# Decay attention and a squared-ReLU feed-forward on one core: the second product of two tiles in seven block products, attention of three tiles in two, and a new order

## The chip, the cores and the metric

The kernel runs on 1 core of one Trainium2 chip. The metric is device time in microseconds of one execution; lower is better. PE is the matrix engine (TensorE), PEld its weight loads, DVE VectorE, ACT ScalarE, POOL GpSimd, SP the engine that issues DMAs.

## What is computed

```python
q, k, v: (4, 8, 768, 64) float32    # batch, heads, sequence, head size
for each block of 64 positions:      # carried state kv_state (batch, head, 64, 64)
    intra = einsum('bhic,bhjc->bhij', qb, kb) * Dmask        # lam**(i-j), lower triangle
    intra = einsum('bhij,bhjd->bhid', intra, vb)
    inter = einsum('bhid,bhde->bhie', qb * lam_pow, kv_state)
    out[block] = intra + inter
    kv_state = lam_block * kv_state + einsum('bhsd,bhse->bhde', kb * rev_pow, vb)
x = out as (3072, 512)               # tokens x (heads * head size)
h = maximum(x @ w_in, 0)             # w_in (512, 2048)
result = (h * h) @ w_out             # w_out (2048, 512)
```

## The kernel before

**Tiles and stages.** The 3072 tokens are 24 chunks of 128 tokens of one sequence, in seven tiles of 2, 3, 3, 4, 4, 4, 4 chunks. For each tile the attention gives x, and the feed-forward part then runs over 16 blocks of 128 hidden features. Values are split into a high and a low part of type fp32r, and a product is three: high by high, high by low, low by high.

**Feed-forward, tiles 0 to 2** (`ffn`, matmuls L633 and L639 to L642): plain products.

**Feed-forward, tiles 3 to 5** (`seven`): eight steps p of two feature blocks. The first product is made of seven block products (L760, 42 matmuls of 128x256 in each step: 2 x 12, then 12 and 6, two block products to a row of twelve) from sums of blocks of x (`combine`, L722 and L725) and sums of blocks of w_in (`sums`, additions on POOL at L696), which are stored in DRAM (`wd`) and streamed back in each step. The second product is plain (L808, 24 matmuls of 128x512 in each step, into four PSUM banks, one for each chunk).

**Feed-forward, tile 6** (`seven2`, `finish`): the first product in the same seven blocks (L875). The second product in seven block products as well (L976, 42 matmuls of 128x256 in each step), except the last step, which is plain in 48 matmuls of 128x256 (L951). The sums of w_out blocks come from `sums2` (L835 to L849) by way of DRAM (`wq`). Seven of the eight PSUM banks hold sums here, so each block product is read out before the next; `finish` (L997) combines the seven sums.

**Attention** (`unit`, `turn_over`): one unit for each chunk. Its *front* (L455, L462) makes the scores and the update of the state; its *values* are the product with the old states (`old64`, L471) and with the masked scores (`values64`, L478). All are matmuls of 64x64, four side by side, recorded as two rows each. One *turn* on PE is the front of a unit and the values of the one before it, as one planned operation. It needs four banks: two for the front (read by DVE at L559 and L565), two for the values, in separate column ranges (read by ACT at L587, added by DVE at L588, multiplied by the decay at L589). In `seven` with its four banks of sums and two of products, a turn takes the place of the product banks, between steps p and p+1 for p = 0, 2, 4, 6 of tiles 3, 4 and 5.

**What sets the order.** Every operation of the program is entered in a `Plan` with an engine, a duration, a key, what it waits for (`deps`), what it only follows (`after`) and the buffers it takes (`SLOTS` gives how many there are of each kind). `Plan.order` lists them by these planned durations, by free buffers and by key, and puts filler matmuls (L321) where PE would be idle before 45 us. A table `EARLY` overrides single keys. The program is then issued in that order on each engine.

Of the kernel before, what the change touches and what calls it, by code (L numbers as in the profile page):

```python
# [19 lines left out]
P = 128  # L20
C = 128
# [17 lines left out]
PLAIN = 3  # L39
Q = 2 * C  # L40
# [19 lines left out]
class Plan:  # L60
# [120 lines left out]

KEY1, KEY2 = (0.0, 3.0), (6.0, 9.0, 14.0)
# [11 lines left out]
POOL_LAT = 2.0  # L194

ISSUE, BEFORE, BEHIND_DMA = 0.45, 1.85, 0.3

EARLY = (
# [28 lines left out]
def kernel(ctx: ExitStack, tc: tile.TileContext, pn, lamx, w, out):  # L227
# [4 lines left out]
    wd = [dram.tile([P, WP], U32, name=f"wd{p}") for p in range(NF // 2)]  # L232
    wdt = [dram.tile([P, 8 * Q], U32, name=f"wq{p}") for p in range(NF // 2)]
# [38 lines left out]
    const.tile([P, 48], F32, name="space")  # L272
# [16 lines left out]
    tiles["ee"] = [t.rearrange("p a b -> p (a b)")[:, 0:DM] for t in tiles["in"]]  # L289
# [241 lines left out]
    def unit(b, c, x, col, key, span, behind=None, vd_act=False, alone=False, raw=None):  # L531

        late = raw is not None or not alone
        t, tv, vd, s1, xr = Buf("in"), Buf("in"), Buf("vds" if late else "half"), [Buf("s1") for _ in range(R)], raw or Buf("xr" if late else "half")
# [41 lines left out]
        def both():  # L576
            old64(t, states, ys)
            values64(vd, s1, ys)

        def back(o_y):  # L580
            def x4(b):
                if raw is None:
                    return at(b).rearrange("p (n i) -> p n i", n=NP)
                i = col // Q * C
                return at(b).rearrange("p (h c i) -> p h c i", h=2, c=NCC)[:, col // C % 2, :, i:i + C]

            oc = [add("ACT", 0.27, 1, lambda r=r: nc.scalar.copy(x4(xr)[:, 2 * r:2 * r + 2], at(ys[r])[:, 0:2 * C].rearrange("p (v i) -> p v i", v=2)), [o_y], [ys[r], xr], f"yi{r}") for r in range(R)]  # L587
            oa = [add("DVE", 0.36, 1, lambda v=v: nc.vector.tensor_tensor(out=by_v(x4(xr), v), in0=y_(ys, v), in1=by_v(x4(xr), v), op=ALU.add), oc, [ys[v], xr]) for v in range(2)]  # L588
            xo = add("DVE", 0.6, 1, lambda: nc.vector.tensor_tensor(out=x4(xr), in0=x4(xr), in1=rdec, op=ALU.mult), oa + o_rdec, [xr])  # L589
            if raw is not None:  # L590
                return [xo]
            cs, n = slice(col, col + C), x.n
            oh = add("ACT", 0.55, 1, lambda: nc.scalar.copy(x_(x, 0, n)[:, :, cs], x4(xr)), [xo], [xr, x])
# [5 lines left out]
        buf_v, dur_v = ys + [t, vd, x or raw, old, mid] + s1, 1.0  # L599
        if alone:  # L600
            o_sc = add("PE", dur_f + EDGE, 0, front, dep_f, buf_f, "sc")
            so = begin_(o_sc)
            return back(add("PE", dur_v + EDGE, 1, both, so + [o_vd] + o_old, buf_v, "y"))
        return dict(key=key, front=Part(dur_f, front, dep_f, buf_f), begin=begin_, values=Part(dur_v, both, [o_vd] + o_old, buf_v), back=back)
# [3 lines left out]
    def rows_out(ti, j, o_done, os_, key):  # L608
# [3 lines left out]
        ob = Buf("vds" if ti >= len(TILES) - 2 and j >= nt - 2 else "ob")  # L612
# [70 lines left out]
    def sums(p, key):  # L683
# [31 lines left out]
    def combine(ti, ready, raw, xc, before, key):  # L715

        A = {n: (lambda i=i: at(raw)[:, 2 * i * Q:2 * (i + 1) * Q]) for i, n in enumerate(("A11", "A12", "A21", "A22"))}
        tmp = Buf("sum")
# [28 lines left out]
    def seven(ti, p, xc, d, os_, key, behind, carry):  # L747

        st, X, Y, u, big, gp = Buf("st"), Buf("bank"), Buf("bank"), Buf("u"), Buf("big"), Buf("gp")
        o_st = plan.op("SP", 5.2, key - 2.5 * 2 * FAST, lambda: nc.sync.dma_start(out=words(at(st)), in_=wd[p]), stored[p], [st], behind + [last_mm.get("stream")])  # L750
# [102 lines left out]
    def seven2(ti, p, xc, d, acc, key, cleared):  # L853
# [6 lines left out]
        for i in range(2):  # L860
            for n in range(1 + p % 2) if not lastp else ():
                m0, m1 = (0, 4) if p % 2 == 0 else ((0, 3), (3, 4))[n]
                o_wt.append(plan.op("SP", 0.36 * (m1 - m0), key - 1.0 * FAST, lambda i=i, n=n, m0=m0, m1=m1: nc.sync.dma_start(
                    out=words(at(wt)[i][n][0]), in_=wdt[p].rearrange("p (a m q) -> p a m q", a=2, m=4)[:, i, m0:m1]), stored2[p], [wt], [o_st] + cleared + last_mm.get("wt", [])))
# [52 lines left out]
        o_12 = tt(0.33, 0.25, lambda: q_(fm, 3), lambda: q_(uq, 3), lambda: q_(bw, 0), ALU.add, [g4], [uq, bw, fm])  # L917
# [69 lines left out]
    def finish(ti, acc, done, key):  # L987

        rows = TILES[ti][0][0] * S + TILES[ti][0][1] * C
        assert [b * S + c * C for b, c in TILES[ti]] == [rows + i * C for i in range(4)]  # L990
        dst = out[rows:rows + 4 * C].rearrange("(i h p) (d m) -> p h d i m", h=2, p=C, d=2)
# [8 lines left out]
        def store(o, b, h, d, i=slice(0, 2)):  # L1000
            plan.op("SP", 0.4 * (i.stop - i.start), key, lambda: nc.sync.dma_start(
                out=dst[:, h, d, i], in_=at(b).rearrange("p (i m) -> p i m", i=2)[:, i]), [o], [b])
# [13 lines left out]
        done[end, 3].after.append(o)  # L1016
# [14 lines left out]
    raws = [Buf("raw") if ti >= PLAIN else None for ti in range(len(TILES))]  # L1031
# [5 lines left out]
    def turn_over(u):  # L1037

        if u is None:
# [152 lines left out]
```

## Time and profile before

| | us |
|---|---|
| three runs | 583.09, 583.12, 583.37 |
| median | 583.12 |
| profiled execution, first to last instruction (span) | 582.5 |
| PE busy | 575.6 |
| VectorE / ScalarE / POOL busy | 435.0 / 266.9 / 29.4 |
| last matmul's end to the span's end, about | 3 |

Of the profiled execution only the span is on hand; the median of the runs is 0.6 us above it. A matmul's row in the trace lasts longer than the distance to the next one, since matmuls overlap; the pace of PE is read from the starts, or from the chain, where overlaps are cut off. The tiles follow one another: the first large product starts at about 19 us, tile 3 at 217, tile 6 at 495.8, and PE's last matmul at about 579.

### The profile page before, as it was taken

The numbers are of one execution on the slowest core, as the hardware profiler recorded it, in microseconds if no ns is written. First come the engines' busy times: TensorE is split into PE (matmuls) and PEld (weight loads), VectorE is DVE, ScalarE is ACT, GpSimd is POOL, SyncE is SP. The second block draws the span as 40 slices with busy tenths as digits, with TensorE's granted clock in tenths as the row PEclk, the third lists the DMA queues.
The fourth block names the chain that finished last, engine by engine and source line by source line (L and its number), as shares of the span: only waits on it lengthen the run. The fifth ranks groups of instructions, "written<-read, shape, count | busy, mean of one in ns | idle before, by whom it ended". The sixth has DMA issues, their size and how long they took to land.

```text
span 582.5 us, 14628 instructions
## 1 busy us (share of the span) xinstructions
PE 575.6 (99%) x6180; PEld 523.3 (90%) x6180; DVE 435.0 (75%) x917; ACT 266.9 (46%) x576; POOL 29.4 (5%) x28
## 2 busy tenths in 40 slices
PE   7999999999999999999999999999999999999997
PEld 6899898889889899888988989889989898999997
DVE  6899999877999786355479667578776548775666
ACT  5887777635434453322235334234442235553452
POOL 2000000100344200000000000000000000000000
PEclk9999999999999999999999999999999999999999
DMA  8846567866788844656454985767777665698722
GB/s 307 278 156 196 188 192 236 280 229 225 272 315 303 341 182 177 214 201 262 181 199 148 362 280 218 274 245 267 255 293 252 231 213 203 198 366 293 260 62 72
DMA packets 36673, 137.26 MB, mean 236 GB/s; under 512 B 3328, under 2 KB 13568, under 8 KB 31488
## 3 DMA queue, kind: packets, MB, share of 16 engines
q1 hardware_dynamic: 36608, 136.34, 66.3%
q8 instruction: 48, 0.79, 0.5%
q14 instruction: 17, 0.14, 0.1%
HBM read 108.01 MB, written 28.31 MB: 234 GB/s over the span
## 4 chain that ended last, share of the span: by engine, by line
PE 94%; DMA 3%; DVE 2%; issue 0%; ACT 0%
PE bank L808 21%; PE bank L760 19%; PE bank L633 15%; PE bank L875 7%; PE bank L976 6%; PE bank L639 5%; PE bank L642 5%; PE bank L640 5%; DMA in<-pn 2%; PE bank L455 2%; PE bank L471 2%; PE bank L478 2%; PE bank L462 1%; DMA halfs<-pn 1%; PE bank L321 1%; PE bank L951 1%
## 5 line engine op out<-in xcount | busy, mean ns | idle before, releaser
L760 PEld LDWEIGHTS bank<-xall,win 128*128 128x128 f32 x1008 | 125.5, 188 | 4.7 <-DVE gs L781 0.7
L808 PE MATMUL bank<-woh,win 128*128 128x512 f32 x384 | 129.0, 394 | 0.0
L760 PE MATMUL bank<-xall,win 128*128 128x256 f32 x1008 | 127.9, 281 | 0.2
L633 PE MATMUL bank<-xall,win 128*128 128x384 f32 (+1 forms) x576 | 93.2, 318 | 0.0
L633 PEld LDWEIGHTS bank<-xall,win 128*128 128x128 f32 x576 | 90.2, 188 | 1.6
L808 PEld LDWEIGHTS bank<-woh,win 128*128 128x128 f32 x384 | 72.0, 188 | 14.6
L808 PE MATMUL bank<-wol,win 128*128 128x512 f32 x192 | 75.2, 392 | 0.0
L639 PE MATMUL bank<-woh,ghs 128*128 128x512 f32 x128 | 50.6, 395 | 0.0
L640 PE MATMUL bank<-wol,ghs 128*128 128x512 f32 x128 | 49.9, 390 | 0.0
L875 PE MATMUL bank<-xall,win 128*128 128x256 f32 x336 | 43.9, 280 | 0.0
L875 PEld LDWEIGHTS bank<-xall,win 128*128 128x128 f32 x336 | 41.6, 188 | 0.2
L808 PEld LDWEIGHTS bank<-wol,win 128*128 128x128 f32 x192 | 36.1, 188 | 5.6
L642 PE MATMUL bank<-woh,gls 128*128 128x512 f32 x128 | 35.9, 392 | 0.5 <-issue 0.5
L792 DVE TENSOR_TENSOR ms<-gs,bank 128x512 f32<-128x512 f32 x24 | 16.5, 686 | 25.6 <-PE bank L760 25.2
L780 ACT COPY gs<-bank 128x256 f32<-128x256 f32 x24 | 9.0, 374 | 57.7 <-PE bank L760 56.1
L649 ACT ACTIVATE gs<-bank 128x384 f32<-128x384 f32 (+1 forms) x48 | 21.9, 455 | 29.3 <-PE bank L633 28.3
L696 POOL TENSOR_TENSOR ms<-win 128x512 f32<-128x512 f32 x16 | 25.2, 1584 | 168.2 <-DVE wol L391 109.4
L799 ACT CAST win<-ms 128x512 fp32r<-128x512 f32 x24 | 14.9, 620 | 40.0 <-DVE ms L798 40.0
L656 DVE TENSOR_TENSOR gls<-gs,ghs 128x384 fp32r<-128x384 f32 (+1 forms) x48 | 28.7, 601 | 5.8 <-ACT ghs L652 5.0
L976 PE MATMUL bank<-woh,win 128*128 128x256 f32 x148 | 32.4, 284 | 0.0
L642 PEld LDWEIGHTS bank<-woh,gls 128*128 128x128 f32 x128 | 23.6, 188 | 5.5 <-issue 0.9
L639 PEld LDWEIGHTS bank<-woh,ghs 128*128 128x128 f32 x128 | 24.0, 188 | 4.9
(144 smaller groups left out, 958.4 us busy)
## 6 DMA issues: line engine op xcount, KB each, us to landing
win<-wd SPq DMA_DIRECT2D x32, 1792.0 KB, 8.3
in<-pn SPq DMA_DIRECT2D x44, 512.0 KB, 6.9
in<-w SPq DMA_DIRECT2D x32, 512.0 KB, 3.9
wd<-xall SPq DMA_DIRECT2D x8, 1024.0 KB, 4.9
out<-obs SPq DMA_DIRECT2D x20, 256.0 KB, 4.0
wd<-win SPq DMA_DIRECT2D x8, 512.0 KB, 6.3
wq<-win SPq DMA_DIRECT2D x7, 512.0 KB, 10.4
wq<-gls SPq DMA_DIRECT2D x7, 512.0 KB, 10.8
```

What stands on the lines that cost most here:

```text
L633: nc.tensor.matmul(at(h)[:, 0:n], wt[:, cc, :], xt[:, cc, 0:n], start=k == 0, stop=k == 3 * NCC - 1)
L639: nc.tensor.matmul(at(os_[j]), gh_()[:, sl], woh[f], start=f == 0, stop=False)
L640: nc.tensor.matmul(at(os_[j]), gh_()[:, sl], wol[f], start=False, stop=False)
L642: nc.tensor.matmul(at(os_[j]), gl_()[:, sl], woh[f], start=False, stop=f == NF - 1)
L649: orr = plan.op("ACT", ta, key - ahead, lambda: nc.scalar.activation(g_(), at(h)[:, 0:n], AF.Relu), [o1], [h, turn_, g])
L656: ogl = plan.op("DVE", tv, key - ahead, lambda: nc.vector.tensor_tensor(out=gl_(), in0=g_(), in1=gh_(), op=ALU.subtract), [og, ogh], [g, g ...
L696: oa = [plan.op("POOL", 1.1, key, lambda f=f, m=m: nc.gpsimd.tensor_tensor(out=at(m), in0=whole(f)[0], in1=whole(f)[1], op=ALU.add), list( ...
L760: nc.tensor.matmul(at(to)[:, i * Q:(i + 1) * Q], wt[a][:, cc, :], xt[b][:, cc, :], start=first and k == 0, stop=stop and k == 5, skip_grou ...
L792: c12 = dve(0.6, 0.7, lambda: nc.vector.tensor_tensor(out=quarter(big, 0, 2).rearrange("p (n i) -> p n i", n=2), in0=quarter(u, 1).unsquee ...
L808: nc.tensor.matmul(at(os_[j]), a, wt[2 * p + k], start=first and part == 0 and wt is woh, stop=p == NF // 2 - 1 and part == 1 and not firs ...
L875: nc.tensor.matmul(at(to)[:, i * Q:(i + 1) * Q], wts[a][:, cc, :], xt[b][:, cc, :], start=i == 0 and k == 0, stop=k == 5, skip_group_check ...
L976: nc.tensor.matmul(at(acc[m])[:, i * Q:(i + 1) * Q], a, block(wn, wp), start=p == 0 and i == 0 and part == 0 and wp == 0, stop=p == NF // ...
```

## The change

1. **Tile 5 takes the form of tile 6.** Tiles from `BOTH2 = 5` on run `seven2` and `finish`. `sums2` therefore moves one tile ahead, to tiles 3 and 4. Tile 6 has its own buffers for x (`raw2`, in the four input buffers) and for a temporary (`sum2`).
2. **Attention of tiles 4, 5, 6 within tiles 3 and 4.** The 12 turns stand behind steps 0, 1, 2, 4, 5, 6 of tiles 3 and 4 (`TURNS`). The results of tiles 5 and 6 go to DRAM (`xd`: eight stores) and come back before their tile (`fetch`: five loads).
3. **Values in one bank.** `values64` adds the product of the masked scores onto the columns that `old64` wrote. It does so in two halves: *straight* (same row half of the array as `old64`, issued with it as an operation of its own) and *cross* (the other row half), issued behind the next unit's front. Between them stands `fence`, a ScalarE copy of 64x2 elements of the bank, which cross waits for. The two copies L587 and the additions L588 go; two multiplications of 128x256 from the banks stay.
4. **Sums of w_in.** The 16 additions of POOL are on DVE.
5. **Order.** Some `after` are `deps` now, a planned DMA latency is longer, and `EARLY` is another table (about a hundred other keys).

```diff
+BOTH2 = 5
+TURNS = [(ti, p) for ti in (3, 4) for p in (0, 1, 2, 4, 5, 6)]
...
+BETWEEN = 0.8
...
-POOL_LAT = 2.0
-
-ISSUE, BEFORE, BEHIND_DMA = 0.45, 1.85, 0.3
+ISSUE, BEFORE, BEHIND_DMA = 0.45, 1.85, 0.5
...
 EARLY = (
-    (2, 0.7), (9, 26.4), (12, 38.4), (36, 22.2), (38, 14.4), (47, 42), (48, -64), (56, 40.4),
+    (3, -59), (6, 56), (7, -6), (14, -1013.1), (22, -723), (26, 183), (30, -1007), (35, -7),
...
-    def values64(vd, s1, ys):
-        for r in range(R):
-            for j in range(2):
-                for v, e in QUARTERS:
-                    i = (2 + r) * C + j * TW
-                    nc.tensor.matmul(
-                        at(ys[v])[half(e), i:i + TW], heads(at(vd))[half(v), head(r, j, e)], s64(s1[r])[half(v), e * 2 + j],
-                        start=False, stop=True, skip_group_check=True)
+    def values64(vd, s1, ys, cross):
+        for j in (1, 0) if cross else (0, 1):
+            for v, e in QUARTERS:
+                r = v ^ cross
+                nc.tensor.matmul(
+                    at(ys[r])[half(e), v * C + j * TW:v * C + j * TW + TW], heads(at(vd))[half(v), head(r, j, e)], s64(s1[r])[half(v), e * 2 + j],
+                    start=False, stop=True, skip_group_check=True)
+
+    def fence(ys, dep, key):
+        o = plan.op("ACT", 0.1, key, lambda: nc.scalar.copy(seen[0:TW], at(ys[1])[0:TW, TW:2 * C:C]), [dep], ys)
+        return o, plan.op("NONE", 0.0, key, lambda: None, [o], lat=-BETWEEN)
...
-            oc = [add("ACT", 0.27, 1, lambda r=r: nc.scalar.copy(x4(xr)[:, 2 * r:2 * r + 2], at(ys[r])[:, 0:2 * C].rearrange("p (v i) -> p v i", v=2)), [o_y], [ys[r], xr], f"yi{r}") for r in range(R)]
-            oa = [add("DVE", 0.36, 1, lambda v=v: nc.vector.tensor_tensor(out=by_v(x4(xr), v), in0=y_(ys, v), in1=by_v(x4(xr), v), op=ALU.add), oc, [ys[v], xr]) for v in range(2)]
-            xo = add("DVE", 0.6, 1, lambda: nc.vector.tensor_tensor(out=x4(xr), in0=x4(xr), in1=rdec, op=ALU.mult), oa + o_rdec, [xr])
+            xo = [add("DVE", 0.36, 1, lambda r=r: nc.vector.tensor_tensor(
+                out=x4(xr)[:, 2 * r:2 * r + 2], in0=at(ys[r])[:, 0:2 * C].rearrange("p (v i) -> p v i", v=2), in1=rdec[:, 2 * r:2 * r + 2], op=ALU.mult), [o_y] + o_rdec, [ys[r], xr]) for r in range(R)]
...
+            if staged is not None:
+                dst = staged.rearrange("p (h n i) -> p h n i", h=2, n=NP)[:, col // C % 2, :, col // Q * C:col // Q * C + C]
+                return [add("SP", 0.75, 1, lambda: nc.sync.dma_start(out=dst, in_=x4(xr)), xo, [xr])]
...
+        first = Part(0.75, straight, [o_vd] + o_old, ys + [t, vd, x or xr, old, mid] + s1)
+        second = Part(0.25, cross, [], ys + [vd] + s1)
...
-        oa = [plan.op("POOL", 1.1, key, lambda f=f, m=m: nc.gpsimd.tensor_tensor(out=at(m), in0=whole(f)[0], in1=whole(f)[1], op=ALU.add),
-                      list(ws[f][0]), [m], lat=POOL_LAT) for f, m in ((f0, ma), (f1, mb))]
+        oa = [plan.op("DVE", 0.6, key, lambda f=f, m=m: nc.vector.tensor_tensor(out=at(m), in0=whole(f)[0], in1=whole(f)[1], op=ALU.add),
+                      list(ws[f][0]), [m]) for f, m in ((f0, ma), (f1, mb))]
...
         if pending:
-            p, so, dest = pending[0]
-            deps, bufs, dur = deps + so + p["values"].deps, bufs + p["values"].bufs, dur + p["values"].dur
...
+            p, so, dest = pending.pop()
+            one, two = p["values"]
+            begun = in_turn("both", plan.op("PE", one.dur, key, one.fn, so + one.deps, one.bufs))
+            fns, deps, bufs, dur = fns + [two.fn], deps + [fence(p["ys"], begun, key)[1 if f else 0]], bufs + two.bufs, dur + two.dur
+        o = in_turn("both", plan.op("PE", dur, key, lambda: [fn() for fn in fns], deps, list({id(b): b for b in bufs}.values())))
...
-            if ti == len(TILES) - 1:
+            if ti >= BOTH2:
```

**PE, one turn in tile 3.** Before, the end of a front (L462) and the start of the values behind it (L471 is `old64`); wide matmuls stand ahead of the front and behind the values alone.

```order
L462 MATMUL bank_83<-halfs,in_97 64x64
L462 MATMUL bank_82<-halfs,in_97 64x64
L462 MATMUL bank_83<-halfs,in_97 64x64
L471 MATMUL bank_81<-in_100,hold_94 64x64
L471 MATMUL bank_79<-in_100,hold_94 64x64
L471 MATMUL bank_81<-in_100,hold_94 64x64
```

Now, the end of the straight half (L470, `values64`), then six matmuls of the plain second product (L812), then the front (L448).

```order
L470 MATMUL bank_86<-s_2_105,halfs 64x64
L470 MATMUL bank_83<-s_3_106,halfs 64x64
L812 MATMUL bank_85<-woh,win 128x512
L812 MATMUL bank_85<-wol,win 128x512
L812 MATMUL bank_84<-woh,win 128x512
L812 MATMUL bank_84<-wol,win 128x512
L812 MATMUL bank_85<-woh,win 128x512
L812 MATMUL bank_84<-woh,win 128x512
L448 MATMUL bank_81<-in_101 64x64
L448 MATMUL bank_88<-in_101 64x64
```

The turn's matmuls, one run before, are two runs now, with six wide matmuls between them.

**DVE, one turn in tiles 3 to 5.** Before: masks of the front (L559), the values (L588, L589), the states (L565, L572), then a weighting (L493), ahead of the next step's first read of a product (L781, not shown).

```order
L800 TENSOR_TENSOR win<-ms,win 128x512
L559 TENSOR_TENSOR s_2_103<-bank_82,mask 128x256
L559 TENSOR_TENSOR s_3_104<-bank_83,mask 128x256
L588 TENSOR_TENSOR halfs<-bank_81,halfs 128x2x128
L588 TENSOR_TENSOR halfs<-bank_79,halfs 128x2x128
L565 TENSOR_TENSOR hold_91<-bank_82,hold_95 128x128
L589 TENSOR_TENSOR halfs<-halfs,rdec 128x4x128
L565 TENSOR_TENSOR hold_91<-bank_83,hold_95 128x128
L565 TENSOR_TENSOR hold_93<-bank_82,hold_91 128x128
L565 TENSOR_TENSOR hold_93<-bank_83,hold_91 128x128
L572 TENSOR_TENSOR hold_93<-hold_93,tables 128x256
```

Now, in tile 3: two multiplications of the values (L587), masks (L556), states (L562, L569), with `sums2` (L841) between.

```order
L804 TENSOR_TENSOR win<-ms,win 128x512
L587 TENSOR_TENSOR obs<-bank_86,rdec 128x256
L587 TENSOR_TENSOR obs<-bank_83,rdec 128x256
L556 TENSOR_TENSOR s_2_105<-bank_81,mask 128x256
L556 TENSOR_TENSOR s_3_106<-bank_88,mask 128x256
L562 TENSOR_TENSOR hold_93<-bank_81,hold_96 128x128
L562 TENSOR_TENSOR hold_93<-bank_88,hold_96 128x128
L562 TENSOR_TENSOR hold_97<-bank_81,hold_93 128x128
L562 TENSOR_TENSOR hold_97<-bank_88,hold_93 128x128
L841 TENSOR_TENSOR obs<-woh,wol 128x512
L569 TENSOR_TENSOR hold_97<-hold_97,tables 128x256
```

The values are read first now, in two operations, and sums of w_out blocks stand among the states.

**PE, from tile 5 to tile 6.** Before: the plain second product of tile 5 (L808, its banks 84, 85, 86, 80), and tile 6's first block products (L875).

```order
L808 MATMUL bank_80<-woh,win 128x512
L808 MATMUL bank_84<-woh,win 128x512
L875 MATMUL bank_79<-xall,win 128x256 x12
L875 MATMUL bank_81<-xall,win 128x256 x12
L875 MATMUL bank_83<-xall,win 128x256 x12
L875 MATMUL bank_82<-xall,win 128x256 x6
L808 MATMUL bank_85<-woh,win 128x512
L808 MATMUL bank_85<-wol,win 128x512
```

Now: the plain last step of tile 5 (L955), the rest of tile 6's first step and the second step's block products (L879), each into a bank of its own, then tile 6's sums (L980).

```order
L955 MATMUL bank_86<-woh,gls 128x256
L955 MATMUL bank_86<-woh,win 128x256
L955 MATMUL bank_86<-wol,win 128x256
L955 MATMUL bank_86<-woh,ghs 128x256
L879 MATMUL bank_83<-xall,win 128x256 x12
L879 MATMUL bank_85<-xall,win 128x256 x6
L879 MATMUL bank_88<-xall,win 128x256 x12
L879 MATMUL bank_87<-xall,win 128x256 x12
L879 MATMUL bank_82<-xall,win 128x256 x12
L980 MATMUL bank_81<-woh,win 128x256
```

The products behind the hand-over take banks that tile 5's sums have just left (83, 85, 88, 87, 82).

## Rows read from the trace of the kernel before

**Rows 1.** The page: busy time by engine; granted clock in 40 slices.
```profile
PE 575.6 (99%) x6180; PEld 523.3 (90%) x6180; DVE 435.0 (75%) x917; ACT 266.9 (46%) x576; POOL 29.4 (5%) x28
...
PEclk9999999999999999999999999999999999999999
```
**Rows 2.** The page: share of engines in the chain that ended last.
```profile
PE 94%; DMA 3%; DVE 2%; issue 0%; ACT 0%
```
**Rows 3.** Stretches (start:end length): PE, PEld, DVE, ACT, POOL busy (x count), clock, DMA.
```profile
100.00:215.00 115.00, 114.54 (x1454) 103.06 (x1453) 98.84 (x207) 52.71 (x110) 25.19 (x16) 1.00 0.77 274
...
310.00:402.00 92.00, 91.88 (x1022) 82.37 (x1021) 65.78 (x141) 35.18 (x73) 0.00 (x0) 1.00 0.74 261
...
509.00:573.00 64.00, 64.00 (x538) 63.94 (x537) 43.08 (x89) 31.25 (x68) 0.00 (x0) 1.00 0.65 226
```
**Rows 4.** Waits of PE's weight loads: releaser, us in total, times, longest.
```profile
PEld bank L455 <- issue: 6.1, 18, 0.4
```
**Rows 5.** The chain in order of time: start us, us, what.
```profile
231.02 2.76 PE bank L808 x12
...
520.60 1.45 PE bank L976 x12
522.04 1.42 PE bank L875 x12
...
573.71 5.77 PE bank L951 x48
```
**Rows 6.** PE's timeline around one turn: start us, us, line, operation, count.
```profile
247.13 0.63 PE L808 MATMUL bank<-woh,win 128*128 128x512 f32 x2
...
248.20 0.65 PE L462 MATMUL bank<-halfs,in 64*64 64x64 f32 x32
248.67 0.65 PE L471 MATMUL bank<-in,hold 64*64 64x64 f32 x32
...
249.71 0.50 PE L808 MATMUL bank<-woh,win 128*128 128x512 f32 x1
250.05 0.40 PE L808 MATMUL bank<-wol,win 128*128 128x512 f32 x1
```
**Rows 7.** The same around a lone front.
```profile
113.74 0.61 PE L642 MATMUL bank<-woh,gls 128*128 128x512 f32 x2
114.28 0.69 PE L455 MATMUL bank<-in 64*64 64x64 f32 x32
...
115.38 0.50 PE L639 MATMUL bank<-woh,ghs 128*128 128x512 f32 x1
115.71 0.39 PE L640 MATMUL bank<-wol,ghs 128*128 128x512 f32 x1
```
**Rows 8.** PE's timeline, start: idle ahead in square brackets; L321 are fillers.
```profile
10.29 0.90 PE L446 MATMUL bank<-s,halfs 64*64 64x128 f32 x32 [0.66 <-DVE s L513]
11.12 0.70 PE L321 MATMUL bank<-obs 128*128 128x256 f32 x2
...
13.66 0.90 PE L432 MATMUL bank<-in 64*64 64x128 f32 x32 [0.94 <-DMA in<-pn]
...
20.53 2.75 PE L321 MATMUL bank<-obs 128*128 128x256 f32 x12
```
**Rows 9.** Groups by line and shape: busy us, mean ns | idle ahead, releaser.
```profile
L696 POOL TENSOR_TENSOR ms<-win 128x512 f32<-128x512 f32 x16 | 25.2, 1584 | 168.2 <-DVE wol L391 109.4 <-DVE xall L705 58.9
...
L588 DVE TENSOR_TENSOR halfs<-bank,halfs 128x256 f32<-128x256 f32 x40 | 15.4, 419 | 3.6 <-ACT halfs L587 3.6
...
L799 ACT CAST win<-ms 128x512 fp32r<-128x512 f32 x24 | 14.9, 620 | 40.0 <-DVE ms L798 40.0
...
L589 DVE TENSOR_TENSOR halfs<-halfs,rdec 128x512 f32<-128x512 f32 x20 | 13.7, 684 | 0.1
...
L587 ACT COPY halfs<-bank 128x256 f32<-128x256 f32 x40 | 12.9, 375 | 16.0 <-PE bank L478 16.0
```

More of the change, by code (lines that the diff above doesn't have):

```diff
@@ L232 @@
     wd = [dram.tile([P, WP], U32, name=f"wd{p}") for p in range(NF // 2)]
+    xd = {ti: dram.tile([P, 4 * 512], F32, name=f"xd{ti}") for ti in range(BOTH2, len(SIZES))}
     wdt = [dram.tile([P, 8 * Q], U32, name=f"wq{p}") for p in range(NF // 2)]
@@ L288 @@
     tiles["fm"] = [flat["m"][:, 0:6 * Q]]
-    tiles["ee"] = [t.rearrange("p a b -> p (a b)")[:, 0:DM] for t in tiles["in"]]
+    tiles["ee"], tiles["raw2"] = ([t[:, k] for t in tiles["in"]] for k in range(2))
+    tiles["raw2"] = [tiles["raw2"]]
+    tiles["sum2"] = [tiles["half"][4]]
     wall = [const.tile([P, NF * DM], F32R, name=n) for n in ("woh", "wol")]
@@ L528, in unit_first, with unit @@
         return oh + ol
-    def unit(b, c, x, col, key, span, behind=None, vd_act=False, alone=False, raw=None):
+    def unit(b, c, x, col, key, span, behind=None, vd_act=False, alone=False, raw=None, staged=None):
         late = raw is not None or not alone
-        t, tv, vd, s1, xr = Buf("in"), Buf("in"), Buf("vds" if late else "half"), [Buf("s1") for _ in range(R)], raw or Buf("xr" if late else "half")
+        far = raw is not None or staged is not None
+        t, tv, vd, s1, xr = Buf("in"), Buf("in"), Buf("vds" if late else "half"), [Buf("s1") for _ in range(R)], raw or Buf("ob" if staged is not None else "xr" if late else "half")
         sc, ys = [Buf("bank") for _ in range(2)], [Buf("bank") for _ in range(2)]
@@ L574, in begin_, with straight, cross @@
             return so + om
-        def both():
+        def straight():
             old64(t, states, ys)
-            values64(vd, s1, ys)
+            values64(vd, s1, ys, 0)
+        def cross():
+            values64(vd, s1, ys, 1)
         def back(o_y):
@@ L602, in unit @@
             so = begin_(o_sc)
-            return back(add("PE", dur_v + EDGE, 1, both, so + [o_vd] + o_old, buf_v, "y"))
-        return dict(key=key, front=Part(dur_f, front, dep_f, buf_f), begin=begin_, values=Part(dur_v, both, [o_vd] + o_old, buf_v), back=back)
+            o = add("PE", first.dur + EDGE, 1, first.fn, so + first.deps, first.bufs, "y")
+            return back(add("PE", second.dur + EDGE, 1, second.fn, [fence(ys, o, key + span)[0]], second.bufs, "y2"))
+        return dict(key=key, ys=ys, front=Part(dur_f, front, dep_f, buf_f), begin=begin_, values=(first, second), back=back)
     last_mm, steps, seconds = {}, {}, {}
@@ L749, in seven @@
         st, X, Y, u, big, gp = Buf("st"), Buf("bank"), Buf("bank"), Buf("u"), Buf("big"), Buf("gp")
[L750 removed]
+        o_st = plan.op("SP", 5.2, key - 2.5 * 2 * FAST, lambda: nc.sync.dma_start(out=words(at(st)), in_=wd[p]), stored[p] + behind, [st], [last_mm.get("stream")])
         last_mm["stream"] = o_st
@@ L987, in finish @@
     def finish(ti, acc, done, key):
-        rows = TILES[ti][0][0] * S + TILES[ti][0][1] * C
-        assert [b * S + c * C for b, c in TILES[ti]] == [rows + i * C for i in range(4)]
-        dst = out[rows:rows + 4 * C].rearrange("(i h p) (d m) -> p h d i m", h=2, p=C, d=2)
+        rows = [b * S + c * C for b, c in TILES[ti]]
         e = [Buf("ee") for _ in range(4)]
@@ L1015, in finish @@
         o = tt(e[3], e[3], 3, [ov], before, slice(Q, 2 * Q))
-        done[end, 3].after.append(o)
+        done[end, 3].deps.append(o)
         store(tt(outs[3], e[3], 3, [ov], end, slice(0, Q)), outs[3], 0, 1, slice(0, 1))
@@ L1030 @@
     xs = [Buf(f"x{ti % 2}") if ti < PLAIN else None for ti in range(len(TILES))]
-    raws = [Buf("raw") if ti >= PLAIN else None for ti in range(len(TILES))]
+    raws = [Buf("raw2" if ti > BOTH2 else "raw") if ti >= PLAIN else None for ti in range(len(TILES))]
     for b_ in xs[:PLAIN]:
@@ L1070, in attention, with fetch @@
             key = begin[ti - 1] + (j - (LEAD if ti < PLAIN else 1.0)) * NF / len(TILES[ti]) * per[ti - 1]
-            if ti - 1 - (j == 0) >= PLAIN:
-                key = begin[ti - 1] + (2 * j - 2) * 2 * FAST + 0.75
-            u = unit(b, c, xs[ti], j * C, key, 0.0 if ti - 1 - (j == 0) >= PLAIN else 4.0, steps[0, BEHIND] if ti == 2 else None, raw=raws[ti])
-            u["last"] = begin[ti - 1] + (len(TILES[ti]) - LEAD) * NF / len(TILES[ti]) * per[ti - 1]
+            late = (ti, j) > (PLAIN + 1, 0)
+            if late:
+                at_, p = TURNS[sum(SIZES[PLAIN + 1:ti]) + j - 1]
+                key = begin[at_] + 2 * p * FAST + 0.75
+            u = unit(b, c, xs[ti], j * C, key, 0.0 if late else 4.0, steps[0, BEHIND] if ti == 2 else None, raw=raws[ti] if ti < BOTH2 else None, staged=xd[ti] if ti >= BOTH2 else None)
+            u["last"] = begin[TURNS[-1][0]] + 2 * TURNS[-1][1] * FAST + 0.75
             so = turn_over(u)
             pending.append((u, so, done_x[ti]))
+    def fetch(ti):
+        key = begin[ti] - 2 * 2 * FAST
+        if raws[ti].kind == "raw":
+            parts = [(lambda: at(raws[ti]), xd[ti])]
+        else:
+            parts = [(lambda i=i: at(raws[ti])[i], xd[ti][:, i * DM:(i + 1) * DM]) for i in range(4)]
+        return [plan.op("SP", 2.9 / len(parts), key, lambda o_=o_, i_=i_: nc.sync.dma_start(out=o_(), in_=i_), done_x[ti], [raws[ti]]) for o_, i_ in parts]
     for ti, cs in enumerate(TILES):
@@ L1082 @@
             attention(3)
-        elif 1 < ti < len(TILES) - 2:
-            attention(ti + 2)
-        elif ti == len(TILES) - 2:
+        elif ti == 2:
+            for t in range(PLAIN + 1, len(TILES)):
+                attention(t)
             turn_over(None)
@@ L1124, in gate @@
         for o in then:
-            o.after.append(g)
+            o.deps.append(g)
     k = SIZES[2] + SIZES[3] + 1
-    for ti in range(PLAIN, len(TILES) - 1):
-        for p in range(0, NF // 2, 2):
-            o, k = turns[k], k + 1
-            o.after.append(steps[ti, p][1])
-            steps[ti, p + 1][0].after.append(o)
-    assert k == len(turns)
+    assert k + len(TURNS) == len(turns)
+    for (ti, p), o in zip(TURNS, turns[k:]):
+        o[0].after.append(steps[ti, p][1])
+        steps[ti, p + 1][0].after.append(o[1])
     gate(["vds"], ["half"])
```

58 lines of the change are left out of this document (29 added, 29 removed), and 36 rows, old and new, of tables (EARLY, SLOTS).

## The prediction

> **What bounds the kernel now.** I read the page's busy times and slices first, then the chain of work that ended last, then stretches of the trace, then single rows of PE. PE is busy 575.6 us of 582.5 at full granted clock [rows 1], and 94% of the chain that ended last is PE [rows 2]. In stretches cut from the middle PE fills 91.88 us of 92.00 and 64.00 of 64.00, while VectorE has 65.78 of 92 and 43.08 of 64 [rows 3]. A busy row alone doesn't say that PE is at its pace, so I looked at starts: identical matmuls follow each other at one constant distance nearly everywhere behind 31 us. The one thing that recurs between them is an idle weight port before the attention's first matmul, 18 times, 6.1 us together, ended by nothing that the trace names [rows 4]. So from 31 us on the time is the sum of PE's own instructions, and the sum below counts PE's rows; other engines' savings count for nothing unless they end a wait of PE, and behind 31 us there is hardly one to end.
>
> **Second product of tile 5.** The chain gives PE's pace without overlaps [rows 5]. Today each of the tile's eight pairs of feature blocks takes 24 matmuls of 128x512, twice the row of twelve: 2 x 2.76 = 5.52 us. By seven block products it takes 42 of 128x256, 3.5 times the row of twelve at 1.45: 5.08 us. Seven pairs go that way: 7 x 0.44 = 3.1 us less. The eighth pair stays plain, in 48 narrower matmuls, 5.77 us instead of 5.52 [rows 5]: 0.25 us more. The first product costs the same in both forms (42 of 128x256). Net on PE: **-2.9 us**. The added VectorE and ScalarE work of this form is what tile 6 has already, where PE never waited [rows 3]; I cost it at nothing under that cover.
>
> The row says that a 256-wide matmul costs 0.121 us and a 512-wide one 0.230, little more than half. The Trainium skill, page "TensorEngine Tiling (Array Packing)", section "Instruction Overhead", puts a fixed 60 cycles on each matmul, which speaks against trading 24 wide ones for 42 narrow ones. By it, at the 2.4 GHz that the granted clock of 1.0 stands for, the seven pairs would save 1.3 us and the eighth would cost 0.6, an estimate of -0.7 in place of -2.9; the trace has the durations themselves and they are shorter, so the rows go into the sum.
>
> **The attention's turns.** A turn's matmuls are 64x64, beside 128-row ones before and behind. One whole turn lies open [rows 6]. From the start of the last two wide matmuls at 247.13 to the second one behind at 250.05 are 2.92 us. Three wide matmuls take 3 x 0.23 = 0.69 of it. The turn's four parts of 32 records follow at 0.47 (248.20 to 248.67): 1.88. Left are 2.92 - 0.69 - 1.88 = 0.35 us that belong to going in and out. Is that a price by turn or by stretch of narrow matmuls? A stretch of half the length, a lone front [rows 7]: 113.74 to 115.71 is 1.97; less 0.69 and 2 x 0.47, 0.34 remain. The price is one of the stretch, not of its length or of what is in it, and the 18 idles of the weight port are its first part.
>
> The trace shows that price, and not its cause; "TensorEngine Tiling (Array Packing)", section "Key Properties", of the Trainium skill has a rule that speaks against this change: switching the tiling mode, not the tile, drains TensorE. It gives no duration, and the sum rests on the rows.
>
> The change cuts each turn in two: old states and straight half of the values first, then front and crossed half, and in the order of PE ordinary matmuls stand between in nearly every turn. Counted over the whole order, stretches of 64-row matmuls between 128-row ones go from 28 to 44. All 16 more lie behind the start, in the part with no slack. 16 x 0.35 = **+5.6 us**. The number of 64x64 matmuls stays the same (1392 in both orders), so nothing comes off against it.
>
> **The small copy and the banks.** The crossed half waits for a ScalarE copy that reads the bank behind the straight half. Behind that wait stand the next wide matmuls on PE. In most turns six wide matmuls (1.38 us) and the front (0.94) are issued between, 2.3 us, against a copy that as a full 128x256 one takes 0.375 [rows 9] behind at most one ScalarE operation in progress (0.62, as L799). In three turns only the front stands there, 0.94 against 0.375 + 0.62. So 0 if ScalarE is where the order puts it; from above, three turns with a few tenths. The next banks are tighter. Behind most turns of tiles 3 and 4 only six wide matmuls now stand before the next block product, where eighteen stood before. The banks of the sums must be read by then: two multiplications of the size of L588, 0.42 each [rows 9], within about 1.6 us. VectorE free: no wait; caught in a 128x512 operation (0.68, as L589): just covered; twice caught: 0.5 us, in up to 12 turns, so 0 to 6 us. VectorE is near 70% busy there [rows 3], and two multiplications replace two copies, two additions and one multiplication, so I take **+0.5 us** in all, near the lower end.
>
> **Start, POOL, DMA.** PE's fillers (matmuls on a zero tile in planned idle time) behind 7 us are four rows with 20 records, two for each instruction, 12 of them in 2.75 us at 20.53 [rows 8]: ten instructions of 0.43 us. The new order has nine: **-0.4 us**. Real idle besides (0.66 at 10.29, 0.94 at 13.66) could go or grow, -1.6 to +1.6; I take 0, since the loads that end it are the same. The 16 additions that leave POOL (25.2 us there [rows 9]) cost VectorE about 16 x 0.6 = 9.6 us in the stretch from 100 to 215, where it has 98.84 of 115 [rows 3]. The shorter turn takes back the 0.68 of L589 [rows 9] in each of eight units, 5.4. That leaves VectorE at about 103 of 115, not the bound. SP gets eight stores and five loads of staged activations more, and the loads of attention inputs now come at six of eight steps instead of every second. They hide behind a turn's period of some 12 us, and stand behind a stream load that may wait for PE; uncovered they would stop PE for whole us. No row of before shows them that dense. I put that into the upper end.
>
> **Sum.** The profiled execution has a span of 582.5 us; the median of the runs is 583.12, 0.6 more. -2.9 + 5.6 + 0.5 - 0.4 = +2.8: span 585.3, median **585.9 us**, 0.5% slower.
>
> **Rivals.** *The price is one of the turn.* If the 0.35 us came once per turn, because the weight port waits for something of the front's (say its inputs), the second stretch would be free, and 583.1 - 2.9 + 0.5 - 0.4 = 580.3, faster. For it: the idle is booked before L455, the front, 18 times [rows 4]. Against it: behind every stretch the way out costs as much as the way in, and it is in the row of the next wide matmul (249.71 to 250.05, 0.34 where 0.23 is the pace) [rows 6], which a wait for inputs can't explain. It decides once fewer than about five of the 16 stretches pay. *The start recovers.* The new order puts 24 block products where before twelve and a long filler stood. If the 1.6 us of real idle went too and no bank were late, 583.1 + 2.7 - 0.4 - 1.6 = 583.8: no change that can be told. For it, the idles are there; against, nine of ten fillers stay planned. *Waits come on top.* VectorE late at twelve turns, or loads late, or the hand-over from tile 5 to tile 6, where seven sums and the next products share eight banks: 3 to 5 us more, 588.5 to 591. For it: only 1.6 us of cover, and tile 5's last sums are read while tile 6 begins. Against: in tile 6 as it stands PE never waits. *It doesn't do what it says*: narrow matmuls cost more in tile 5 than in tile 6, and the 2.9 us stay away: 588.8. Against it: nothing in the rows makes a matmul's pace hang on the tokens that it works for. By the page's 60 cycles, with -0.7, it would be 588.1.
>
> **How the numbers follow.** Forecast 0.60 (584.3 to 587.5); price by turn 0.08; start recovers 0.14; waits on top 0.15; no saving 0.03. A measurement of this kernel tells 0.2% (1.2 us) from no change. Faster is the first rival, 0.08. The same is the second with the low edge of the forecast, 0.16. Slower is the rest, 0.76. The range leaves out the faster case, part of the recovered start and the top of the waits: 583.3 to 589.0.
>
> **What would show it.** In the profile after: PE's rows at the second product of tile 5 at 0.121 us apart; about 36 stretches of 64x64 matmuls behind 31 us, each with 0.35 us around it, and some 33 idles of the weight port before them where 18 were; both parts of one turn together some 0.35 us longer than 2.23; no PE row that waits for the small copy; the block products of tiles 3 and 4 at unchanged pace. Wrong would be: a second stretch without its 0.35, PE idles at the turns with VectorE or a DMA as releaser, a hand-over between tiles 5 and 6 with idle PE, or first wide matmuls at another time than now by more than 1.6 us.

## The result and the profile after

The changed kernel took 587.89 us (median of 4 runs, 587.25 to 590.01) against 583.16 (4 runs): ratio 1.0084, interval 1.0065 to 1.0103. That is 4.7 us slower, where 2.8 was forecast: inside the range, and just above the 584.3 to 587.5 of the main forecast. Measured again in a later set of runs (**after_again** below), it was 586.86 against 583.65 (1.0060, 1.0038 to 1.0082): 3.2 us slower.

The page after: busy time by engine, then the engines' shares of the chain that ended last.

```profile
PE 577.3 (99%) x6328; PEld 528.5 (90%) x6328; DVE 449.6 (77%) x972; ACT 268.4 (46%) x586; POOL 4.2 (1%) x12
...
PE 82%; DMA 7%; DVE 6%; ACT 3%; issue 1%; SPq 0%; ACTq 0%
```

The span is 585.5 us, 3.0 more than before. PE is as busy as in [rows 1], but only 82% of the chain is PE where it was 94% [rows 2]: somewhere PE now waits for a DMA by way of VectorE.

**The saving is there.** The chain in tile 5 and at its end (start us, us, what):

```profile
474.37 1.42 PE bank L879 x12
475.78 1.45 PE bank L980 x12
...
498.67 5.76 PE bank L955 x48
```

These are the durations that the sum took from tile 6 [rows 5], so 7 x 0.44 - 0.25 = 2.8 us less work. Nothing in tile 5, or at the hand-over to tile 6, opens PE's stream. Two stretches (start:end length; PE, PEld, DVE, ACT, POOL busy; clock; DMA):

```profile
100.00:215.00 115.00, 114.70 (x1455) 101.34 (x1454) 93.41 (x212) 47.17 (x103) 0.00 (x0) 1.00 0.75 268
...
430.00:494.00 64.00, 64.00 (x540) 64.00 (x539) 45.97 (x94) 33.29 (x70) 0.00 (x0) 1.00 0.82 287
```

The first also shows that moving POOL's 16 additions to VectorE cost PE next to nothing: PE still fills 114.70 of 115 us. VectorE even fell from 98.84 us [rows 3] to 93.41, below the 103 of the prediction. The difference lies in VectorE's other operations. In the kernel before, some of them took up to three times as long while POOL was adding, as the first of these two L656 did beside the POOL row, and the second not:

```profile
145.06 3.25 POOL L696 TENSOR_TENSOR ms<-win 128x512 f32<-128x512 f32 x2 [27.52 <-DVE xall L705]
...
147.26 1.47 DVE L656 TENSOR_TENSOR gls<-gs,ghs 128x384 fp32r<-128x384 f32 x1
...
149.30 0.56 DVE L656 TENSOR_TENSOR gls<-gs,ghs 128x384 fp32r<-128x384 f32 x1
```

From 100 to 215 us, seven of the 21 L656 of this shape overlap a POOL addition and take 1.12 us on average, the other 14 take 0.55, as all 19 do now. With L655, L705 and L572, which show the same, that had cost VectorE about 9 us, most of the 10.5 that the additions cost it now.

**The cuts cost what the stretches said.** PE's timeline around one turn of tile 3 (start us, us, line, operation, count), two stretches of narrow matmuls with six wide ones between:

```profile
237.41 0.69 PE L464 MATMUL bank<-in,hold 64*64 64x64 f32 x32
237.92 0.41 PE L470 MATMUL bank<-s,halfs 64*64 64x64 f32 x16
238.26 0.50 PE L812 MATMUL bank<-woh,win 128*128 128x512 f32 x1
238.60 0.40 PE L812 MATMUL bank<-wol,win 128*128 128x512 f32 x1
...
239.87 0.69 PE L448 MATMUL bank<-in 64*64 64x64 f32 x32
...
241.19 0.50 PE L812 MATMUL bank<-woh,win 128*128 128x512 f32 x1
241.53 0.40 PE L812 MATMUL bank<-wol,win 128*128 128x512 f32 x1
```

From the first narrow matmul to the second wide one are 238.60 - 237.41 = 1.19 us: 48 records of 0.0147 (0.71), one wide at 0.23, and 0.25 for the way out. The second stretch has 80 records: 1.66 - 1.18 - 0.23 = 0.25 again. The way in, ahead of the first row, adds 0.09. I did this for every stretch behind 40 us, from the starts: 20 before cost 6.7 us, 36 now cost 12.0. A stretch costs 0.33 to 0.35 whatever its length, and the cuts cost 5.3.

**PE waits a little more.** Waits of PE from 100 to 425 us (releaser, us in total, times, longest):

```profile
PE bank L764 <- DVE gs L785: 1.7, 2, 1.3
PE bank L643 <- ACT ghs L656: 0.3, 1, 0.3
PE bank L764 <- DVE ms L788: 0.3, 1, 0.3
```

There were 0.5 us of them before. The chain ahead of the longest:

```profile
340.51 8.30 DMA in<-pn
...
348.83 0.69 DVE halfs L489
349.57 0.69 DVE obs L841
350.26 0.34 DVE gs L785
...
350.64 0.95 PE bank L764 x6
```

An attention load issued at 340.51 lands 8.30 us later. L489, the weighting of the values, waits for it at the head of VectorE's queue. Behind it stand L841 (a sum of w_out blocks) and L785, which empties the bank that PE needs. VectorE's waits at L489's load before (L493 there) and after:

```profile
DVE halfs L493 <- DMA in<-pn: 16.3, 9, 2.7
```
```profile
DVE halfs L489 <- DMA in<-pn: 7.0, 8, 1.6
```

VectorE stood longer at late loads before, and PE did not notice. A likely reason is the thinner cover, six wide matmuls behind most turns; no run varies the cover alone.

So the two profiled executions differ by -2.8 (second product), +5.3 (cuts), about +1.5 (waits, from PE's starts) and about -1.1 (start): 2.9, against 3.0 in the spans.

The last two terms belong to this one execution. The trace of after_again, the same program, has the same span of 585.5 us and the same cost of the cuts, but hardly a wait of PE from 100 to 425 us:

```profile
PE bank L764 <- DVE gs L785: 0.4, 1, 0.4
PE bank L764 <- DVE ms L788: 0.3, 1, 0.3
```

From its starts, the waits are about -0.5 against the kernel before, and the start is +1.0. The saving and the cuts are the same in both traces; waits and start are not.

### The profile page after: what moved, and what is told of

Same layout as the page of the kernel before. It is cut to its first block, busy times and chain, and to the rows that moved or that the text cites. A ratio compares the mean times of both kernels' runs of the same rounds, so it can differ in the third digit from the quotient of the medians.

```text
span 585.5 us, 15039 instructions
## 1 busy us (share of the span) xinstructions
PE 577.3 (99%) x6328; PEld 528.5 (90%) x6328; DVE 449.6 (77%) x972; ACT 268.4 (46%) x586; POOL 4.2 (1%) x12
## 4 chain that ended last, share of the span: by engine, by line
PE 82%; DMA 7%; DVE 6%; ACT 3%; issue 1%; SPq 0%; ACTq 0%
PE bank L812 14%; PE bank L879 14%; PE bank L980 12%; PE bank L764 12%; PE bank L637 11%; DMA in<-pn 4%; PE bank L643 4%; PE bank L646 4%; PE bank L644 4%; DMA in<-w 2%; PE bank L464 2%; PE bank L955 2%; PE bank L448 2%; PE bank L470 1%; PE bank L455 1%; DMA halfs<-pn 1%
## 5 line engine op out<-in xcount | busy, mean ns | idle before, releaser
L637 PE MATMUL bank<-xall,win 128*128 128x384 f32 (+1 forms) x576 | 95.7, 320 | 0.0
L812 PE MATMUL bank<-woh,win 128*128 128x512 f32 x256 | 88.1, 400 | 0.0
L879 PE MATMUL bank<-xall,win 128*128 128x256 f32 x672 | 86.1, 280 | 0.0
L879 PEld LDWEIGHTS bank<-xall,win 128*128 128x128 f32 x672 | 82.6, 188 | 0.2
L980 PE MATMUL bank<-woh,win 128*128 128x256 f32 x296 | 64.5, 284 | 0.0
L812 PEld LDWEIGHTS bank<-woh,win 128*128 128x128 f32 x256 | 48.0, 188 | 10.6
L980 PE MATMUL bank<-wol,win 128*128 128x256 f32 x184 | 52.1, 283 | 0.0
L812 PE MATMUL bank<-wol,win 128*128 128x512 f32 x128 | 50.4, 393 | 0.0
L980 PEld LDWEIGHTS bank<-woh,win 128*128 128x128 f32 x296 | 50.2, 191 | 0.0
L934 ACT CAST win<-ms 128x512 fp32r<-128x512 f32 (+1 forms) x48 | 25.3, 536 | 25.8 <-DVE ms L913 19.3
L980 PEld LDWEIGHTS bank<-wol,win 128*128 128x128 f32 x184 | 35.0, 190 | 0.0
L900 DVE TENSOR_TENSOR ms<-gs,bank 128x512 f32<-128x512 f32 (+1 forms) x32 | 17.3, 551 | 18.6 <-PE bank L879 18.4
L374 ACT ACTIVATE ms<-in 128x512 f32<-128x512 f32 x32 | 21.6, 676 | 18.6 <-DMA in<-w 9.4
L784 ACT COPY gs<-bank 128x256 f32<-128x256 f32 x16 | 6.0, 372 | 50.7 <-PE bank L764 50.7
```

What stands on the lines that cost most here:

```text
L374: o = add("ACT", 0.58, lambda: nc.scalar.activation(at(m), words(1).bitcast(F32), AF.Abs), [o], [st, m])
L637: nc.tensor.matmul(at(h)[:, 0:n], wt[:, cc, :], xt[:, cc, 0:n], start=k == 0, stop=k == 3 * NCC - 1)
L812: nc.tensor.matmul(at(os_[j]), a, wt[2 * p + k], start=first and part == 0 and wt is woh, stop=p == NF // 2 - 1 and part == 1 and not firs ...
L879: nc.tensor.matmul(at(to)[:, i * Q:(i + 1) * Q], wts[a][:, cc, :], xt[b][:, cc, :], start=i == 0 and k == 0, stop=k == 5, skip_group_check ...
L900: return plan.op("DVE", dur, key + dk, lambda: nc.vector.tensor_tensor(out=out_(), in0=a(), in1=b(), op=op), deps, bufs)
L934: oh = act(dur[0], dk, lambda: nc.scalar.copy(gq_(0, at_, n), src()), deps, bufs + [gq])
```

## The experiments

Theory: PE pays about 0.35 us for each stretch of 64-row matmuls, 16 more of them outweigh a real saving, and late loads add to it. Rivals: the price is one of the turn; the added loads and stores are what costs; the saving isn't real.

**unsplit**: the turn made whole again, with the small copy issued from within it.

```diff
-            begun = in_turn("both", plan.op("PE", one.dur, key, one.fn, so + one.deps, one.bufs))
-            fns, deps, bufs, dur = fns + [two.fn], deps + [fence(p["ys"], begun, key)[1 if f else 0]], bufs + two.bufs, dur + two.dur
+            begun = plan.op("NONE", 0.0, key, lambda: None, so + one.deps)
...
+            fns, deps, bufs, dur = [one.fn] + [copy] + fns + [two.fn], deps + [begun], bufs + one.bufs + two.bufs, dur + one.dur + two.dur
```

> The changed kernel with every turn issued on PE as one operation: old states, straight half, small copy, front, crossed half, with no wide matmul between; everything else as changed. Stretches of 64-row matmuls go from 44 to 28. Theory 1 (each stretch costs 0.35 us, whatever is in it): 16 x 0.35 = 5.6 us less than the changed kernel's 587.9, so 582.3; up to 1.5 us more if banks are late, since the turn now needs its four banks at once (583.8). Theory 2 (the time is lost to the loads and stores that were added, not to the cuts): the cuts give nothing back, 587 to 588. PE waits for the small copy in neither theory: the front's 0.94 us stand between.

588.57 us (586.54 to 590.44) against 583.74: 1.0086 (1.0067 to 1.0105). A miss: it is no faster than the changed kernel, as theory 2 had it. Its starts show why. The 20 stretches behind 40 us are back, but new waits stand in and beside them. (The traced execution is the longest of the six.) PE's waits from 100 to 425 us:

```profile
PE bank L643 <- ACT ghs L656: 1.7, 4, 0.6
PE bank L470 <- issue: 1.6, 1, 1.6
PE bank L764 <- DVE ms L788: 1.2, 2, 0.9
PE bank L464 <- DVE ms L796: 1.0, 1, 1.0
...
PE bank L470 <- ACT space L1058: 0.3, 1, 0.3
```

The undivided turn needs four banks at once, and the table of keys had been made for the divided one. The last line is the small copy where no front stands between, at the last turn: the crossed half starts 0.68 us behind the straight half's start, which lasts 0.24. Everywhere else in this trace the front covers it.

**before_split**: the opposite, on the kernel before. Front and values of a turn are two PE operations. Wide matmuls then stand between them in twelve turns, two in tile 2 and ten in tiles 3 to 5.

```diff
-        o = in_turn("both", plan.op("PE", dur, key, run, deps, list({id(b): b for b in bufs}.values())))
+        o = in_turn("both", plan.op("PE", dur, key, (f.fn if f else pending[0][0]["values"].fn), deps, list({id(b): b for b in bufs}.values())))
...
+            o.dur -= p_["values"].dur
...
+            back_o = plan.op("PE", p_["values"].dur, key + SPLIT, p_["values"].fn, pending[0][1] + p_["values"].deps, list(vb), [o])
```

> The kernel before with one edit: in tiles 3 to 5 the front and the values of a turn are two operations on PE, with wide matmuls of the second product between. Stretches go from 28 to 40, nothing else is added or removed. Theory 1 (price by stretch): 583.1 + 12 x 0.35 = 587.3, perhaps 0.9 less where banks come free earlier (586.4). Theory 2 (price by turn, or none): 583.1 within 0.3, or less.

587.14 us against 583.74: 1.0059 (1.0047 to 1.0071), 3.4 us slower with no instruction added. One of its turns on PE:

```profile
247.44 0.65 PE L464 MATMUL bank<-halfs,in 64*64 64x64 f32 x32
248.02 0.50 PE L810 MATMUL bank<-woh,win 128*128 128x512 f32 x1
248.36 0.40 PE L810 MATMUL bank<-wol,win 128*128 128x512 f32 x1
...
251.52 0.65 PE L480 MATMUL bank<-s,halfs 64*64 64x64 f32 x32
252.10 3.09 PE L762 MATMUL bank<-xall,win 128*128 128x256 f32 x24
```

The front now has a way out of its own, 0.34 from the first wide start to the second, as in [rows 6, 7], and the values stand alone 4 us later. From the starts, the 12 more stretches cost 4.2 us; some 1.7 us of short waits, most at block products, went, as the lower expectation had it. The price by turn is refuted.

**weigh_later**: L489 of the late turns is issued later on VectorE, at most 3.5 us (`AHEAD_OF`) of planned time ahead of the turn that uses it. In VectorE's order it moved in eight of twelve, two of them by two operations only.

```diff
+    for o in weigh:
+        user = min((q for q in done if o in q.deps), key=lambda q: q.start)
+        done.remove(o)
+        done.insert(next(i for i, q in enumerate(done) if q is user or q.start > max(o.start, user.start - AHEAD_OF)), o)
```

> The changed kernel with one step moved on VectorE: the weighting of the values (L489, which waits for an attention load) is issued up to some 6 us later in six of the twelve late turns, so that the combining of block products is not queued behind it. Theory 1 (PE's idles of 1.4 and 0.6 us at L764 come from VectorE standing at a late load): they go, 587.9 - 2.0 = 585.9, and single runs differ by less than the 2.8 us seen. Theory 2 (the late loads then stop the front instead): no gain, 587.9, with PE idle before L448.

586.14 us (584.55 to 590.01), 1.0050 (1.0029 to 1.0071), and VectorE's waits at this load went from 7.0 us to 0.5. PE's waits from 100 to 425 us are now

```profile
PE bank L767 <- DVE gs L788: 0.4, 1, 0.4
PE bank L767 <- DVE ms L791: 0.3, 1, 0.3
```

The front doesn't wait instead. These are 0.7 us of waits where the first trace of the changed kernel has 2.3, but the second, after_again's, has 0.7 too, with 3.9 us of VectorE's waits at this load. The times don't decide it either: the interval overlaps both of the changed kernel's (1.0065 to 1.0103 and 1.0038 to 1.0082). So the edit takes away VectorE's waits at the load; that it saves PE time is not shown. The spread between runs did not shrink, so it has another cause. **unsplit_later** has both edits.

> Both edits of the two kernels unsplit and weigh_later on the changed kernel. Theory 1: both add up, 582.3 - 2.0 = 580.3, below the kernel before (583.1). If the late loads only move their wait: 582.3.

587.68 us, 1.0071 (1.0053 to 1.0088): neither 580.3 nor 582.3. Nothing adds up while the undivided turns wait for banks.

**after_again**, the changed kernel in the next set of runs, with the result given at the top.

> The changed kernel unaltered, for a measurement beside the others on one chip and one set of runs of the kernel before. Both theories: about 4.7 us above the kernel before, single runs 2 to 3 us apart.

**plain_tile6** prices the first part of the change alone, by taking it away from tile 6 of the kernel before. The keys of `EARLY` that name operations from tile 6 on are left out as well.

```diff
-            if ti == len(TILES) - 1:
+            if False:
                 used = []
```

> The kernel before with the opposite of the change's first part: tile 6 takes the plain second product too (24 matmuls of 128x512 in each step in place of 42 of 128x256, and its last 48 of 128x256 gone); its result leaves by the plain way out, and the sums of w_out blocks are not made. Theory 1 (a 128x256 matmul costs 0.1205 us, a 128x512 one 0.2296, nothing else): 7 x 0.44 - 0.25 = 2.8 us slower than the kernel before. Theory 2 (the narrow form has a cost that the distance of starts doesn't show, or its VectorE work costs PE time): slower by 1 us or less, or not at all.

587.23 us against 583.65: 1.0058 (1.0040 to 1.0076), 3.6 us slower. At the pace of its rows PE has 3.1 us more to do, and the plain way out is longer: 4.1 us from PE's last matmul to the end where it was 3.0. Theory 1 holds.

**unsplit_order** and **unsplit_order2**: the instructions of unsplit, with more keys added to `EARLY`. They come from a search over keys that counted 0.345 us for each stretch and let loads land up to 2 us behind the plan.

> The kernel unsplit with another table of keys behind 100 us, worked out so that VectorE, the loads and the banks are ready when the undivided turns stand on PE (the price of a stretch and late loads counted in the plan). Same instructions, 28 stretches. Theory 1 (the 5.6 us of the 16 stretches are real, and in unsplit only new waits of PE at the turns ate them): the waits of PE behind 100 us fall below 2 us, and it is 4 to 6 us faster than the changed kernel, so level with the kernel before or up to 1.5 us below it. Theory 2 (a long stretch costs as much as two short ones, by its instruction issue or otherwise): no faster than unsplit.

> A second such table, found apart from the first, to see whether the result hangs on one order. Theory 1: within 1 us of unsplit_order. Theory 2: like unsplit.

unsplit_order: 583.80 us (581.36 to 586.07) against 583.65, ratio 1.0000 (0.9983 to 1.0016). It is 3.1 us faster than after_again in the same set, though not 4 to 6 us. All the added loads and stores are still in it, so they are not what these 3.1 us were lost to. From the starts, the stretches cost 5.4 us less than in after_again, the start 1.3 less, and PE's waits some 2.8 more. No such search was run for the divided kernel, so the times alone don't tell what a new order is worth without the whole turns. unsplit_order2 took 585.97 (1.0036, 1.0020 to 1.0052), 2.2 us more than the first: a miss; the result does hang on the order. In unsplit_order PE's waits from 100 to 425 us, 2.7 us in all where less than 2 was expected, are

```profile
PE bank L886 <- DVE ms L910: 1.4, 3, 0.7
PE bank L886 <- DVE gs L907: 0.5, 1, 0.5
PE bank L592 <- issue: 0.5, 1, 0.5
PE bank L592 <- ACT space L1180: 0.3, 1, 0.3
```

and the chain ahead of one of them is the known one, a load, then its weighting (L611 here), then the reading of a bank:

```profile
286.27 6.32 DMA in<-pn
...
292.62 0.69 DVE halfs L611
293.31 0.34 DVE ms L910
...
293.70 1.33 PE bank L886 x9
```

**order_later** is unsplit_order with the edit of weigh_later (six weightings are moved, not seven); **order_loads** has a third table, for later loads.

> unsplit_order with the edit of weigh_later: in seven of the twelve late turns the weighting of the values (which waits for an attention load) is issued later on VectorE. In unsplit_order's trace three idles of PE at L886, 0.67, 0.90 and 0.50 us, stand behind a VectorE that waits at such a load. Theory 1 (it is the place in VectorE's queue that costs, not the load): they go, 583.8 - 2.0 = 581.8, 0.3% below the kernel before. Theory 2 (the undivided turn then waits for the load itself): 583.8.

> unsplit with a third table of keys, worked out as in unsplit_order but with attention loads taken to land up to 3 us later. Theory 1: the three idles at late loads go or shrink, 582 to 583. Theory 2: 583.8 as unsplit_order.

order_later: 582.61 us (580.64 to 585.83) against 583.49, ratio 0.9995 (0.9977 to 1.0012). The three idles went, as PE's waits from 100 to 425 us show:

```profile
PE bank L594 <- ACT space L1183: 0.9, 2, 0.6
PE bank L889 <- DVE ms L913: 0.4, 1, 0.4
PE bank L889 <- DVE obs L712: 0.2, 1, 0.2
```

A late small copy has come instead: at one turn it stands behind two ScalarE casts of 0.62 us, and PE waits 0.6 us for it although a front stands between. Six of its twelve runs lie at 580.6 to 581.7, below all 23 of the kernel before (582.2 to 584.7); the other six lie at 583.6 to 585.8. By its interval it is level with the kernel before and not clearly apart from unsplit_order. order_loads: 583.57 (1.0000, 0.9981 to 1.0018), no better than unsplit_order.

**What separates the runs** may in part be the start. I took PE's time at 40 us, less the time that its work up to then would take at its pace. The three traces with the old start lie within 1.2 us (18.2 to 19.4), the nine of the changed kernel and its variants between 17.6 and 21.5. In three of the nine PE stops amid identical narrow matmuls, released by nothing that the trace names. The rows of one, after_again:

```profile
25.40 0.45 PE L448 MATMUL bank<-in 64*64 64x64 f32 x17
26.82 0.40 PE L448 MATMUL bank<-in 64*64 64x64 f32 x12 [0.97 <-issue]
```

In these three the second 16 KB transfer of the queue that carries instructions starts at 19.1 to 19.4 us, in the other six at 15.8 to 17.2. That points to late instructions; which engine the transfer serves the trace doesn't tell, and I didn't test it.

The granted clock has a part too. In order_loads PE stood 1.46 us at 29.6 to 31.0. About 2 us later the clock fell to its lower level, 1.2 GHz (the 0.50 in the last line), and matmuls of 128x512 followed each other at 0.43 us instead of 0.23 until about 36.3:

```profile
31.02 0.33 PE L591 MATMUL bank<-s,halfs 64*64 64x64 f32 x4 [1.46 <-issue]
...
32.93 0.63 PE L764 MATMUL bank<-woh,ghs 128*128 128x512 f32 x1
33.36 0.63 PE L765 MATMUL bank<-wol,ghs 128*128 128x512 f32 x1
...
33.00:34.00 1.00, 1.00 (x4) 0.81 (x3) 1.00 (x3) 0.81 (x2) 0.00 (x0) 0.50 0.91 315
```

That is about 1.5 us lost. unsplit has stops of 1.2 and 1.5 us near the same time and keeps 1.00. Of the 76 runs of the changed kernel and its variants, thirteen have a mean granted clock of 0.997 or less, most of them among the longest of their kernel; no run of the kernel before, where its clock is on record, lies under 0.999. The rest of the spread, such as the two groups of order_later, stays open.

## Why the prediction came out as it did

- **Second product, -2.9**: right. The rows of tile 5 are those of tile 6, and plain_tile6 shows the value from the other side. The Trainium skill's fixed cost per matmul ("TensorEngine Tiling (Array Packing)", "Instruction Overhead"), which would have left 0.7, is not seen here in that size: its 60 cycles would be 0.025 us at 2.4 GHz, an estimate. Twelve matmuls of 128x256 still take 1.45 us and twelve of 128x512 take 2.76 [rows 5], so what each matmul costs beyond its columns is (2 x 1.45 - 2.76) / 12, about 0.01 us.
- **16 stretches, +5.6**: right in count and price. 5.3 us from the starts in this kernel, 4.2 us for 12 in before_split. The forecast of 33 idles of the weight port was off: the trace books 25 to it, the rest of the price being visible in the starts alone. That the price is one of switching agrees with the Trainium skill's "Key Properties" on the same page; the cause of the price no run here shows.
- **Small copy, 0**: right in the changed kernel, where no PE row waits for it. In the undivided turns it cost 0.4 us at the one turn without a front, and 0.6 in order_later at a turn with one: the few tenths that the prediction gives as the case from above.
- **Waits, +0.5**: misplaced, and not one number. They were about +1.5 in one trace and -0.5 in the other. The longest came not from the two multiplications behind the turns but from L489 at a late load. I had loads stopping PE by themselves in the upper end; here the load stopped VectorE's queue, and by it PE.
- **VectorE, 103 of 115 us**: 10 us too high. The prediction counted the additions at 0.6 us (they took 0.69) and left out that VectorE's own operations had been slower beside POOL's. It changes nothing in the sum, since VectorE was not the bound.
- **Fillers and start, -0.4**: not a constant. The profiled executions give -1.1, after_again's +1.0 on the same instructions.
- **The base, 0.6 between span and time**: wrong. In every run that lists both, the time is 1.7 us above the span, the kernel before included (583.1 with 581.4). So the profiled execution of before (582.5) was not the median one but 1.1 us slower, and that of the changed kernel lies 0.6 us below its median. Between the spans the sum was right to 0.2 us (+2.8 for +3.0); the 1.1 and the 0.6 are the rest of the 4.7. That it came so close is luck: +1.0 in the waits and -0.7 in the start cancelled in one trace, and -1.0 and +1.4 in the other.
- **Rivals**: the price by turn fell, by the rows and by before_split. Waits on top came in part and in one trace, from a late load as that rival says, but by way of VectorE's queue. The recovered start came in some executions only.

## What to carry to other kernels

Count how often the matrix engine changes between kinds of matmul in its final order, and price a change from the rows around one; here 16 of them cost twice what a cheaper product saved, and an order made without that price cuts freely. Where VectorE empties the banks, look for an operation that waits for a load ahead of one that frees a bank: everything behind it waits too. Issuing it later took VectorE's waits there from 7.0 us to 0.5 and from 8.4 to 0.9; a gain in time clear of noise was not shown. Take more than one trace of a kernel before a wait is priced. Undoing the cuts alone gave nothing back here, where banks and keys were set up for them; it paid with an order made anew with the price in it, and with one such order more than with the other.

## What the runs showed that I had not expected

Narrow matmuls ran into stops of 0.5 to 1.6 us with no releaser, mostly at the same instruction of a program (the thirteenth record of L470's sixteen near 30 us, and again near 326 to 334 us; after_again and unsplit also stop at L448 near 26 us). One trace of the changed kernel has such stops and the other has none. Whole turns suffer from it in unsplit (1.6 us) and unsplit_order (0.5); the kernel before, with 128 records in a turn too, shows one such idle of 0.5 us, between wide matmuls.
